# Row sums' reciprocals scheduled apart from GpSimd, and 32-bit value products for eight heads in the fills' PSUM banks

## The chip, the cores and the metric

The kernel runs on one core of one Trainium2 chip. The metric is the device time of one execution in microseconds; the kernel before is timed in three runs, and one execution of it is profiled. The engines are named as in the profile: PE (TensorE's matmuls) and PEld (its weight loads), DVE (VectorE), ACT (ScalarE), POOL (GpSimd), SP (SyncE, which issues the DMAs).

## The reference

Three layers follow one another: an attention with a decay per key, a mixture of eight experts whose gates are normalised by rows and columns, and a dense layer pair. All is in 32-bit floats.

```
# q, k, v: (4, 8, 576, 64); f: (4, 8, 576); 32 heads in all
scores = (q @ k.T) / 8 + cum[:, None] - cum[None, :]      # cum = cumsum(log(clip(f))), causal mask
attn   = exp(scores - rowmax);  attn /= attn.sum(-1) + 1e-9
x      = concat_heads(attn @ v)                           # (2304, 512)
P      = exp(x @ w_gate - max); 8 times: rows, then columns normalised     # (2304, 8)
x      = sum over e of P[:, e] * (relu(x @ w1[e]) @ w2[e])                 # w1: 512x1024, w2: 1024x512
h      = x @ w_in;  out = max(0.01 * h, h) @ w_out                         # 512x2048, 2048x512
```

## The kernel before

**Two stages.** The first 321 us or so are the head stage: 32 heads of attention, two heads (a pair) sharing a few steps. From there on PE runs the experts' and the dense layers' products in an order that a second planner writes out; that is the main stage. Products of the first experts on the tokens of the first heads, the *fills*, are already put between the heads' steps, four matmuls at a time (first layer L203, second layer L230). They go into the two PSUM banks of the pool `ps_m`.

**Precision.** Most products are split: an operand x is stored as a rounded high part hi (type fp32r) and a low part x - hi, and the product is made of two or three fast matmuls. "Native" products take the 32-bit values as they are, at more PE time a matmul.

**The steps of a head.** DVE casts q and k to their high parts (L393, L387), GpSimd makes the low parts (L398, L390). Scores go into the four banks of `ps_s` in six pieces (L441, L442). DVE masks each piece and takes the row minimum (L453, L457); ScalarE makes the exponentials with their row sums (L466). PE transposes the probabilities into the two banks of `ps_t` (L492); ScalarE copies them out (L499), and for split heads DVE subtracts to get the low part `ptl` (L508). The value product (`pv`, L528) comes in two pieces of columns, 0 to 255 and 256 to 575, into a bank of `ps_s`. For heads 0 to 9 (`n < EARLY`) it is native, with v as loaded (`rv`); for the others v is split (`vp`: DVE cast L423, GpSimd low part L425), and the product leaves the terms for ScalarE's copy (L549) and DVE's addition (L556) to join. Native heads need one ScalarE copy (L545).

**The reciprocal.** For a pair, `recip` (L570 to L572) runs three small DVE operations on the row sums: an addition on 96x2, the addition of 1e-9 on 128x10, a reciprocal on 128x10. GpSimd spreads the result (`rb`, L577), PE transposes that, DVE multiplies it onto the pair's output `xs` (L592), ScalarE and GpSimd split it (L607, L611), and the gate product follows (L637, L638). GpSimd also makes the low parts of the fills' weights (L164).

**The order.** `head_events` and the loop over the fills list every step with its engine, a duration in microseconds, a delay, what it needs, which PSUM ring it takes and when it is due. `run_heads` then walks a clock of its own and puts the steps of each engine into an order. The engine letters are M for PE, A for ScalarE, V for DVE, P for GpSimd, D for the DMA queue. A step marked "VP" runs on DVE and, like every step of GpSimd, is placed only where this clock has the other of the two engines free of such steps; a step marked "V" is placed without regard to GpSimd:

```
if how[0] in ("VP", "P"):
    s_ = max(s_, port["P" if e == "V" else "V"])
```

The casts (k1, q1, vp) are marked "VP", the reciprocal (rc) "V". The clock lives in the planner alone; on the chip each engine runs its own order and waits only for data and free buffers.

Of the kernel before, what the change touches and what calls it, by code (L numbers as in the profile page):

```python
# [10 lines left out]
F32 = mybir.dt.float32  # L11
# [9 lines left out]
P = 128  # L21
B, H, S, D = 4, 8, 576, 64
# [44 lines left out]

EARLY = 10
HEAD_E = dict(
# [25 lines left out]
def moe_kernel(ctx, tc, qT, kT, v, fg, w_gate, w1, w2, w_in, w_out, out):  # L95
# [198 lines left out]
    with ExitStack() as actx:  # L294
# [120 lines left out]
        def v_split(n, op):  # L415
            if n < EARLY:
                return
            rv = rvs[(n // 2) % 2]
            if op == "vp":
                vps[n] = a2.tile([P, 5, 4 * D], F32R, tag="vp", name="vp")  # L420
            vv = vps[n].rearrange("p j (s d) -> p j s d", d=D)
            if op == "vp":
                nc.vector.tensor_copy(vv[:, :, 0:4:3, :], rv)  # L423
            else:
                nc.gpsimd.tensor_tensor(  # L425
                    vv[:, :, 1:3, :], rv, f(vv[:, :, 0:4:3, :]), ALU.subtract)
# [54 lines left out]
        def tr(n, u):  # L481
            if n < EARLY:
                if n not in pts:
                    pts[n] = (a2.tile([P, PTW], F32, tag="pth", name="pt"),)
            elif n not in pts:
                pts[n] = (a2.tile([P, PTW], F32R, tag="pth", name="pth"),
                          a2.tile([P, PTW], F32R, tag="ptl", name="ptl"))
            ps = ps_t.tile([P, 512], F32, tag="t", name="ps_t")
            for j, qs, c in TPLAN[u]:
                for i in qs:  # L490
                    m = QT[i][1]
                    nc.tensor.transpose(  # L492
                        ps[:KV[j], c:c + m], prb[n, i][:m, j * P:j * P + KV[j]], ident[:m, :m])
                    c += m
            tps[n, u] = ps
# [6 lines left out]
        def tr_lo(n, u):  # L502
            if n < EARLY:
                return
            hi, lo = pts[n]
            for r, c0, c1, o in TEV[u]:
                w = slice(o, o + c1 - c0)
                nc.vector.tensor_tensor(  # L508
                    lo[:r, w], tps[n, u][:r, c0:c1], f(hi[:r, w]), ALU.subtract)
# [5 lines left out]
        def pv(n, r):  # L515
            ra, rb = RG[r]
            ps = ps_s.tile([P, 512], F32, tag="s", name="ps_pv")
            js = [j for j in range(5) if (QT[j][0] if j == 4 else j * P) < rb]
            todo = [(j, s) for j in js for s in pts[n]]
            for x, (j, s) in enumerate(todo):  # L520
                q0 = 480 if j == 4 else j * P
                a = max(ra, q0)
                o = PTOFF[j] + a - q0
                if n < EARLY:
                    vp = rvs[(n // 2) % 2][:KV[j], j].rearrange("p h d -> p (h d)")
                else:
                    vp = vps[n - n % 2].rearrange("p j (h c) -> p j h c", h=2)[:KV[j], j, n % 2]
                nc.tensor.matmul(  # L528
                    ps[:, a - ra:rb - ra], vp, s[:KV[j], o:o + rb - a],
                    start=(x == 0), stop=(x == len(todo) - 1))  # L530
            pvs[n, r] = ps
# [7 lines left out]
        def pv_copy(n, r):  # L539
            ra, rb = RG[r]  # L540
            me, ot = halves(n)
            if n // 2 not in xss:
                xss[n // 2] = a2.tile([P, S], F32, tag="xs", name="xs")
            if n < EARLY:
                nc.scalar.activation(  # L545
                    xss[n // 2][me, ra:rb], pvs.pop((n, r))[me, 0:rb - ra], AF.Copy)
                return
            xts[n, r] = a2.tile([P, 320], F32, tag="xt", name="xt")
            nc.scalar.activation(xts[n, r][me, 0:rb - ra], pvs[n, r][ot, 0:rb - ra], AF.Copy)  # L549

        def pv_add(n, r):
            if n < EARLY:
                return
            ra, rb = RG[r]
            me, ot = halves(n)
            nc.vector.tensor_tensor(  # L556
                xss[n // 2][me, ra:rb], pvs.pop((n, r))[me, 0:rb - ra],
                xts.pop((n, r))[me, 0:rb - ra], ALU.add)
# [97 lines left out]
        TE, TL = 6.9, 8.6  # L656
        base_of = [TE * min(n, EARLY) + TL * max(n - EARLY, 0) for n in range(NH + 8)]
        hvs = {}
        BUFS = dict(s=4, t=2, m=2, xt=2)

        def place(n, off):
            x = n + off
            k = int(x)
            return base_of[k] + (x - k) * (base_of[k + 1] - base_of[k]) if x > 0 else x * TE
# [24 lines left out]
        def head_events(n):  # L689
            early, pair = n < EARLY, n - n % 2  # L690
            T = HEAD_E if early else HEAD_T
# [11 lines left out]
            if n % 2 == 0:  # L703
                PT_ = PAIR_E if early else PAIR_T
                if n:
                    hv(("vload", n), ("D", 1.1, 2.0), v_load, n,
                       need=[("vl", n - 4)] + [("pv", n - m, r) for m in (4, 3) for r in range(2)])
                if not early:
# [4 lines left out]
            for x in (0, 1, 2, 3, 4, 5):  # L713
                hv(("qk", n, x), ("M", M_QK[x], 0.17), qk, n, x,
                   need=[(k, n) for k in ("rows", "k1", "k2", "q1", "qd", "q1l")]
                   + [("pv", n - 3, r) for r in range(2)],
                   ring="s", rel=[("ex", n, x), ("mn", n, x)], due=place(n, T[f"qk{x}"]))
                hv(("mn", n, x), ("V", V_MN[x], 0.12), qk_min, n, x,
# [15 lines left out]
            for r in range(2):  # L734
                hv(("pv", n, r), ("M", ((0.65, 2.4) if early else (0.44, 1.5))[r], 0.2), pv, n, r,
                   need=[(lo, n, u) for u in ((0, 1), (0, 1, 2, 3))[r]]
                   + [("vload", pair), ("vl", pair)],
                   ring="s", rel=[("cp" if early else "ad", n, r)], due=place(n, T[f"pv{r}"]))
                xfree = [(k, pair - 4) for k in ("xd", "xl")]
# [4 lines left out]
            if n % 2 == 0:  # L744
                return
            n, last = pair, "cp" if early else "ad"
            T = PT_ = PAIR_E if early else PAIR_T
            hv(("rc", n), ("V", 0.5, 0.1), recip, n,
               need=[("ex", n + y, x) for y in range(2) for x in range(6)])
# [11 lines left out]
            for r in range(2):  # L761
                hv(("ga", n, r), ("M", 0.3, 0.17), gate, n, r, need=[("xl", n), ("wg",)],
                   ring="t", rel=[("gb", n, r)], due=place(n, T[f"ga{r}"]))
                hv(("gb", n, r), ("V", 0.4, 0.07), gate_add, n, r, need=[("ga", n, r), ("gb", n - 2, r)])

# [7 lines left out]
        for x, (dur, fns) in enumerate(fills):  # L773
            for fn in fns:
# [22 lines left out]
                else:  # L797
# [7 lines left out]
                    if q == 0:  # L805
                        fowner = ("low", j, b, c) if not l2_ else ("end", j, b, c)
                    F = ("f", x)
                    hv(F, ("M", 0.88 if l2_ else 0.71, 0.2), fill_main, x, fn, need=list(dict.fromkeys(need)),
                       ring="m" if q == 0 else None, rel=[fowner], due=1e6 + x)
# [17 lines left out]
        def run_heads():  # L827
# [14 lines left out]
            must = set(rest)  # L842
            free = dict(M=0.0, A=0.0, V=0.0, P=0.0, D=0.0)
            port = dict(V=0.0, P=0.0)
# [13 lines left out]
            stop, owed = None, set()  # L858
            while must or owed:
                best = None  # L860
# [45 lines left out]
                if not must and not owed and fills[stop][1][0].args[3] < 2:  # L906
                    owed |= {fmain[stop + 1]} | set(fside[stop + 1])
                for y in succ[x]:
# [975 lines left out]
```

## Time and profile before

| | us |
|---|---|
| median of three runs (lowest, highest) | 2042.12 (2039.62 to 2042.59) |
| the profiled execution's own time | 2041.69 |
| its span, first to last instruction | 2039.9 |
| PE busy | 1996.0 (98%) |
| PEld busy | 1947.4 (95%) |
| DVE busy | 1767.0 (87%) |
| ACT busy | 981.2 (48%) |
| POOL busy | 1163.1 (57%) |

The shares are means over both stages; the stages differ, so each is read by itself. The span is 1.8 us shorter than the execution's own time. Matmuls overlap and their ends are modelled, so a busy PE is not a PE at its peak.

### The profile page before, as it was taken

Reading aid. Unit: us, or ns where it says so; the run is one execution under the profiler, and the core shown is the slowest. Engines: PE = TensorE matmul, PEld = TensorE weight load, DVE = VectorE, ACT = ScalarE, POOL = GpSimd, SP = SyncE. Lnnn points to the kernel's source line nnn. Section 1 sums busy time; section 2 is a strip of 40 time slices with the busy share of each in tenths; the row PEclk is TensorE's granted clock in tenths of the full one; section 3 lists DMA queues with packets and bytes.
Section 4 is the critical chain, followed back from the end, with each engine's and each line's share of the span. In section 5 each row is a group of like instructions: output and inputs, shape, how many; then the busy total and the mean of one; then the engine's idle time right before and its main releaser. Section 6 shows DMA issues by size and latency. Waiting matters only on the chain.

```text
span 2039.9 us, 32131 instructions
## 1 busy us (share of the span) xinstructions
PE 1996.0 (98%) x11600; PEld 1947.4 (95%) x11600; DVE 1767.0 (87%) x2426; ACT 981.2 (48%) x1752; POOL 1163.1 (57%) x731
## 2 busy tenths in 40 slices
PE   7999899999999999999999999999999999999999
PEld 5788788999999999999999999999999999999998
DVE  6799897688889999998989989889898988888766
ACT  6877675454444334433343343334334346655443
POOL 5667556446665657666566646656575564455302
PEclk9999999999999999999999999999999999999999
DMA  5645437567887767786767777777777755767563
GB/s 142 164 136 159 129 104 245 214 244 247 280 305 269 257 233 255 240 273 238 240 243 256 256 246 245 255 243 249 242 266 244 250 215 191 259 233 238 179 210 139
DMA packets 145622, 460.54 MB, mean 226 GB/s; under 512 B 15912, under 2 KB 42168, under 8 KB 145464
## 3 DMA queue, kind: packets, MB, share of 16 engines
q1 hardware_dynamic: 145460, 458.48, 66.8%
q8 instruction: 93, 1.52, 0.3%
q14 instruction: 65, 0.53, 0.1%
q10 hardware_dynamic: 4, 0.00, 0.0%
HBM read 402.76 MB, written 51.08 MB: 222 GB/s over the span
## 4 chain that ended last, share of the span: by engine, by line
PE 85%; DVE 8%; ACT 2%; DMA 2%; issue 2%; POOL 0%; SPq 0%; DVEq 0%; ACTq 0%; POOLq 0%
PE x L1382 43%; PE y L1382 32%; PE ps_pv L528 1%; PE ps_m L230 1%; PE ps_t L492 1%; PE y L230 1%; PE y L203 1%; DVE ps_s L453 1%; PE ps_s L441 1%; PE x L203 1%; PE x L230 1%; PE ps_s L442 1%; ACT p L466 1%; DVE hl L1453 1%; PE ps_m L203 1%
## 5 line engine op out<-in xcount | busy, mean ns | idle before, releaser
L1382 PE MATMUL x<-xw,w 128*128 128x384 f32 x2676 | 501.0, 335 | 2.7 <-DVE xw L1136 1.4
L1382 PE MATMUL x<-hh,w 128*128 128x384 f32 x1792 | 491.1, 334 | 2.7 <-DVE w L1204 1.7
L1382 PEld LDWEIGHTS x<-xw,w 128*128 128x128 f32 x2676 | 466.9, 188 | 4.9 <-DVE xw L1136 2.0
L1382 PE MATMUL y<-xw,w 128*128 128x384 f32 x2004 | 375.0, 335 | 0.9 <-DVE u L1424 0.9
L1382 PE MATMUL y<-hh,w 128*128 128x384 f32 x1344 | 368.1, 334 | 0.0
L1382 PEld LDWEIGHTS y<-xw,w 128*128 128x128 f32 x2004 | 349.5, 188 | 1.6 <-DVE u L1424 1.4
L1204 POOL TENSOR_TENSOR w<-wr,w 128x512 fp32r<-128x512 f32 x161 | 255.7, 1592 | 165.4 <-ACT w L160 152.7
L1382 PEld LDWEIGHTS x<-hh,w 128*128 128x128 f32 x1792 | 326.7, 188 | 3.6 <-DVE w L1204 2.4
L1382 PE MATMUL x<-hl,w 128*128 128x384 f32 x896 | 299.7, 335 | 0.9 <-DVE hl L1453 0.9
L1382 PEld LDWEIGHTS y<-hh,w 128*128 128x128 f32 x1344 | 245.2, 188 | 0.3 <-issue 0.3
L1382 PE MATMUL y<-hl,w 128*128 128x384 f32 x672 | 224.8, 334 | 0.0
L1465 DVE TENSOR_TENSOR acc_C<-x,acc_C 128x768 f32<-128x768 f32 x177 | 168.3, 951 | 32.3 <-PE x L1382 30.6
L1465 DVE TENSOR_TENSOR acc_C<-y,acc_C 128x768 f32<-128x768 f32 x148 | 140.9, 952 | 57.6 <-PE y L1382 56.1
L160 ACT ACTIVATE w<-wr 128x512 fp32r<-128x512 f32 x288 | 175.2, 622 | 28.6 <-PE y L1382 17.4
L1382 PEld LDWEIGHTS x<-hl,w 128*128 128x128 f32 x896 | 168.3, 188 | 1.5 <-DVE hl L1453 1.5
L1449 ACT ACTIVATE hh<-u 128x768 fp32r<-128x768 f32 x91 | 77.1, 847 | 142.4 <-PE y L1382 82.1
L1449 ACT ACTIVATE hh<-spare 128x768 fp32r<-128x768 f32 x84 | 71.1, 847 | 148.4 <-PE x L1382 62.6
L1449 ACT ACTIVATE hh<-k 128x768 fp32r<-128x768 f32 x112 | 94.9, 847 | 89.3 <-PE x L1382 50.2
L1382 PEld LDWEIGHTS y<-hl,w 128*128 128x128 f32 x672 | 126.1, 188 | 0.2 <-DVE hl L1453 0.2
L1449 ACT ACTIVATE hh<-c 128x768 fp32r<-128x768 f32 x70 | 59.3, 846 | 123.5 <-PE y L1382 83.4
L1418 ACT ACTIVATE u<-x 128x768 f32<-128x768 f32 x91 | 74.1, 814 | 92.0 <-PE x L1382 84.6
L1453 POOL TENSOR_TENSOR hl<-k,hh 128x768 fp32r<-128x768 f32 x35 | 69.0, 1973 | 83.3 <-ACT hh L1449 83.3
(253 smaller groups left out, 3848.8 us busy)
## 6 DMA issues: line engine op xcount, KB each, us to landing
xw<-xo_t SPq DMA_DIRECT2D x208, 768.0 KB
xw<-xo_b SPq DMA_DIRECT2D x154, 768.0 KB
wr<-in_w_dram SPq DMA_DIRECT2D x88, 512.0 KB
pb<-prow SPq DMA_DIRECT2D x44, 384.0 KB
xo_t<-xw SPq DMA_DIRECT2D x16, 768.0 KB
rq<-in_qT_dram SPq DMA_DIRECT2D x64, 144.0 KB
rk<-in_kT_dram SPq DMA_DIRECT2D x64, 144.0 KB
xo_b<-xw SPq DMA_DIRECT2D x12, 768.0 KB
```

The source lines that it names most:

```text
L160: nc.scalar.activation(hv, src, AF.Copy)
L203: nc.tensor.matmul(ps, w_[:, fs], x_[k][:, xs], start=(x == 0), stop=(x == 11))
L230: nc.tensor.matmul(ps, h_[:, ts], w_, start=(x == 0), stop=(x == 11))
L441: nc.tensor.matmul(o, q1[:, q0:q0 + m], k1[:, k0:k9], start=True, stop=False)
L442: nc.tensor.matmul(o, q2[0:D + 4, q0:q0 + m], k2[0:D + 4, k0:k9], start=False, stop=True)
L453: nc.vector.tensor_tensor_reduce(o, o, mask[:m, w:w + k9 - k0], scale=-SCALE, scalar=3e38, op0=ALU.add, op1=ALU.min, accum_out=mn)
L1204: ENG[e].tensor_tensor(lo, blk(g, which, WSRC[which][n]), f(hi), ALU.subtract)
L1382: nc.tensor.matmul(o_, w[:, k, w_], m[:, k, :], start=a and k + y == 0, stop=z and k == 1 and y == 2, skip_group_check=True)
L1418: nc.scalar.activation(ctile(u, name, name, bufs), pview(u, p), AF.Copy)
L1449: nc.scalar.activation(hi, tmp[u, LSRC[l]], AF.Copy)
L1453: ENG[e].tensor_tensor(lo, tmp[u, LSRC[l]], f(hi), ALU.subtract)
L1465: nc.vector.tensor_tensor(a, pview(u, l), a, ALU.add)
```

## The change

Five things are edited. `rc` becomes a "VP" step. The set of native heads becomes 0 to 7 (`NATIVE`), and their value products take a bank of `ps_m`, the fills' ring, where they took one of `ps_s`. The planner's numbers move: the fills' matmul steps cost 0.94 and 0.77 where they cost 0.88 and 0.71, the DMA queue and head 0's scores start at 1.5, the gate steps of the pairs that straddle two token parts get unequal durations. The need of `vload` is rewritten for pairs whose forerunner has no low part. And the loop goes on until a fill product is whole, so that the head stage ends on one.

```
-EARLY = 10
+NATIVE = (0, 1, 2, 3, 4, 5, 6, 7)
...
         def pv(n, r):
             ra, rb = RG[r]
-            ps = ps_s.tile([P, 512], F32, tag="s", name="ps_pv")
+            ps = ps_m.tile([P, 512], F32, tag="m", name="ps_m") if n in NATIVE else \
+                ps_s.tile([P, 512], F32, tag="s", name="ps_pv")
...
-                       need=[("vl", n - 4)] + [("pv", n - m, r) for m in (4, 3) for r in range(2)])
+                       need=[("pv", n - m, r) for m in (4, 3) for r in range(2)] if n - 4 in NATIVE
+                       else [("vl", n - 4)])
...
-                   ring="s", rel=[("cp" if early else "ad", n, r)], due=place(n, T[f"pv{r}"]))
+                   ring="m" if early else "s", rel=[("cp" if early else "ad", n, r)], due=place(n, T[f"pv{r}"]))
...
-            hv(("rc", n), ("V", 0.5, 0.1), recip, n,
+            hv(("rc", n), ("VP", 0.5, 0.1), recip, n,
...
-                    hv(F, ("M", 0.88 if l2_ else 0.71, 0.2), fill_main, x, fn, need=list(dict.fromkeys(need)),
+                    hv(F, ("M", 0.94 if l2_ else 0.77, 0.2), fill_main, x, fn, need=list(dict.fromkeys(need)),
...
-            free = dict(M=0.0, A=0.0, V=0.0, P=0.0, D=0.0)
+            free = dict(M=0.0, A=0.0, V=0.0, P=0.0, D=1.5)
...
-            while must or owed:
+            idle = []
+            while True:
+                if not must and not owed:
+                    if fills[stop][1][0].args[3] == 2:
+                        break
+                    owed |= {fmain[stop + 1]} | {m for m in fside[stop + 1] if m not in over}
```

Since the planner decides the order, these edits move instructions on every engine in the head stage. From the experts' first products on, PE's order is the same. Seven lines are added ahead of and among these functions, so that line numbers after the change are larger by one around `recip` (L571 to L573) and by seven in the main stage.

On DVE, around the reciprocal of the pair of heads 14 and 15: the cast of the next q (L393) stands right ahead of it, with one multiplication between.

```order
L453 ISA ps_s,st<-ps_s,mask 96x288
L453 ISA st 96x1
L393 CAST q_2042<-rq 128x576
L592 TENSOR_TENSOR xs<-xs,ps_r 128x320
L570 TENSOR_TENSOR st<-st 96x2
L571 TENSOR_SCALAR st<-st 128x10
L572 RECIPROCAL st<-st 128x10
L508 TENSOR_TENSOR ptl<-ps_t,pth 128x96
```

The same place in the changed kernel:

```order
L387 CAST k_2078<-rk 128x576
L508 TENSOR_TENSOR ptl<-ps_t,pth 128x512
L453 ISA ps_s,st<-ps_s,mask 96x512
L453 ISA st 96x1
L649 TENSOR_TENSOR lgT<-ps_g,lgT 16x384
L571 TENSOR_TENSOR st<-st 96x2
L572 TENSOR_SCALAR st<-st 128x10
L573 RECIPROCAL st<-st 128x10
L423 CAST vp<-rv_193 128x5x2x64
L508 TENSOR_TENSOR ptl<-ps_t,pth 128x96
```

The reciprocal now stands a subtraction, a masked minimum and a gate addition behind the last cast, which is that of k, and a cast of v follows it.

On GpSimd, the operations ahead of the spread (rb) of the same pair, before the change:

```order
L164 TENSOR_TENSOR w<-wr,w 128x512 x3
L398 TENSOR_TENSOR q_2042<-rq,q_2042 64x576
L611 TENSOR_TENSOR xp<-xs,xp 128x192
L611 TENSOR_TENSOR xtl<-xs,xth 128x384
L577 COPY rb<-st 128x640
L565 MEMSET st 128x30
L390 TENSOR_TENSOR k_1_228<-rk,k_2043 64x576
```

And in the changed kernel:

```order
L612 TENSOR_TENSOR xp<-xs,xp 128x192
L612 TENSOR_TENSOR xtl<-xs,xth 128x384
L398 TENSOR_TENSOR q_2077<-rq,q_2077 64x576
L164 TENSOR_TENSOR w<-wr,w 128x512
L390 TENSOR_TENSOR k_1_228<-rk,k_2078 64x576
L578 COPY rb<-st 128x640
L425 TENSOR_TENSOR vp<-rv_193,vp 128x5x128
L566 MEMSET st 128x30
L398 TENSOR_TENSOR q_2197<-rq,q_2197 64x576
```

The output's low part (xp, xtl) has moved ahead of the q low part, and the k low part from behind the spread to right ahead of it.

On PE, the value product of head 8 between the scores of head 9, before the change:

```order
L528 MATMUL ps_pv<-pt,rv_193 128x256
L528 MATMUL ps_pv<-pt,rv_193 128x128
L441 MATMUL ps_s<-k_1016,q_1015 128x384
L442 MATMUL ps_s<-k_1_228,q_1_226 128x384
L586 MATMUL ps_r<-ident,rb 128x128
L586 MATMUL ps_r<-ident,rb 128x96 x2
L492 MATMUL ps_t<-ident,p_1177 128x96
L492 MATMUL ps_t<-ident,p_1177 64x96
L441 MATMUL ps_s<-k_1016,q_1015 96x512
L442 MATMUL ps_s<-k_1_228,q_1_226 96x512
L528 MATMUL ps_pv<-pt,rv_193 128x320 x3
```

And in the changed kernel:

```order
L441 MATMUL ps_s<-k_1007,q_1006 128x384
L442 MATMUL ps_s<-k_1_228,q_1_226 128x384
L441 MATMUL ps_s<-k_1007,q_1006 96x512
L442 MATMUL ps_s<-k_1_228,q_1_226 96x512
L587 MATMUL ps_r<-ident,rb 128x128 x2
L529 MATMUL ps_pv<-pth,vp 128x256
L529 MATMUL ps_pv<-ptl,vp 128x256
L529 MATMUL ps_pv<-pth,vp 128x128
L529 MATMUL ps_pv<-ptl,vp 128x128
L587 MATMUL ps_r<-ident,rb 128x128
L587 MATMUL ps_r<-ident,rb 128x96 x2
L529 MATMUL ps_pv<-pth,vp 128x320
```

Head 8's product is now split into high and low parts, and all scores of head 9 stand ahead of it. Counted in the same two orders, the first-layer fill products ahead of head 12 are 28 in the changed kernel and 8 before; ahead of head 15 both have 48 of the first and 16 of the second layer; at the end of the head stage 192 stand against 204 of the first layer, and 144 of the second in both. None stands ahead of head 10 in either.

## Rows read from the trace of the kernel before

**Rows 1.** Windows by stage: length, busy us (instructions) by engine, clock, DMA share, GB/s.

```profile
20.00:96.00 76.00, 70.17 (x424) 57.10 (x422) 56.45 (x176) 57.49 (x189) 43.29 (x40) 0.98 0.53 144
96.00:321.00 225.00, 210.39 (x1363) 187.95 (x1362) 199.92 (x579) 163.64 (x478) 140.39 (x121) 0.98 0.47 133
321.00:2040.00 1719.00, 1706.49 (x9776) 1694.77 (x9776) 1497.76 (x1635) 749.09 (x1057) 969.89 (x552) 1.00 0.70 242
```

**Rows 2.** PE's waits, 20:96, 96:210 and 210:325 us: total us, times, longest.

```profile
PE ps_pv L528 <- ACT p L466: 4.7, 4, 2.0
...
PE ps_t L492 <- DVE ptl L508: 6.8, 5, 2.2
...
PE ps_t L492 <- DVE ptl L508: 4.0, 3, 2.1
PE ps_s L441 <- DVE xs L556: 2.3, 3, 1.7
```

**Rows 3.** DVE's groups by form, 20 to 310 us: count, busy us, mean ns.

```profile
L571 DVE TENSOR_SCALAR st<-st 128x10 f32<-128x10 f32 x16 | 14.3, 894 | 3.1 <-ACT p L466 1.9
...
L570 DVE TENSOR_TENSOR st<-st 96x2 f32<-96x2 f32 x16 | 13.9, 870 | 0.0
```

**Rows 4.** Timeline of 202 to 208 us: start, us, instruction, idle before.

```profile
202.23 1.42 POOL L398 TENSOR_TENSOR q<-rq,q 64x576 fp32r<-64x576 f32 x1 [0.55 <-ACT xth L607]
...
202.44 1.22 DVE L570 TENSOR_TENSOR st<-st 96x2 f32<-96x2 f32 x1
...
203.72 1.42 POOL L611 TENSOR_TENSOR xtl<-xs,xth 128x576 fp32r<-128x576 f32 x1
203.76 1.41 DVE L571 TENSOR_SCALAR st<-st 128x10 f32<-128x10 f32 x1
...
206.68 0.89 PE L492 MATMUL ps_t<-ident,p 128*128 128x128 f32 x7 [1.74 <-DVE ptl L508]
```

**Rows 5.** DVE's timeline, 183.5 to 187 us.

```profile
183.94 0.15 DVE L570 TENSOR_TENSOR st<-st 96x2 f32<-96x2 f32 x1
184.19 0.17 DVE L571 TENSOR_SCALAR st<-st 128x10 f32<-128x10 f32 x1
```

**Rows 6.** Windows around the first and the last of four slow stretches.

```profile
43.30:47.00 3.70, 3.60 (x14) 2.95 (x15) 1.90 (x8) 3.12 (x13) 0.00 (x0) 0.69 0.29 83
286.00:290.00 4.00, 4.00 (x22) 3.90 (x21) 3.10 (x11) 2.46 (x9) 1.69 (x2) 0.64 0.05 19
```

**Rows 7.** PE's timeline: a native value product, then first and last of a split one.

```profile
92.27 0.92 PE L528 MATMUL ps_pv<-pt,rv 128*128 128x256 f32 x4
93.94 2.52 PE L528 MATMUL ps_pv<-pt,rv 128*128 128x320 f32 x10
...
111.70 0.28 PE L528 MATMUL ps_pv<-pth,vp 128*128 128x256 f32 x1
...
111.99 0.28 PE L528 MATMUL ps_pv<-ptl,vp 128*128 128x128 f32 x1
113.97 0.31 PE L528 MATMUL ps_pv<-pth,vp 128*128 128x320 f32 x1
...
115.29 0.27 PE L528 MATMUL ps_pv<-ptl,vp 64*128 64x96 f32 x1
```

**Rows 8.** DVE's groups of split heads, 96 to 321 us.

```profile
L508 DVE TENSOR_TENSOR ptl<-ps_t,pth 128x480 fp32r<-128x480 f32 (+4 forms) x108 | 49.6, 489 | 3.0 <-ACT pth L499 2.4
L556 DVE TENSOR_TENSOR xs<-ps_pv,xt 64x256 f32<-64x256 f32 (+1 forms) x44 | 19.7, 451 | 2.2 <-ACT xt L549 1.5
L423 DVE CAST vp<-rv 128x640 fp32r<-128x640 f32 x10 | 8.1, 810 | 2.3 <-DMA rv<-in_v_dram 2.0 <-issue 0.3
```

**Rows 9.** Windows of the pairs of heads 8, 18 and 20, between their first scores.

```profile
72.25:87.86 15.61, 14.67 (x93) 12.09 (x92) 11.22 (x38) 13.31 (x43) 12.76 (x12) 1.00 0.63 174
163.16:183.01 19.85, 18.57 (x125) 16.62 (x124) 18.86 (x57) 15.69 (x47) 15.20 (x15) 1.00 0.45 130
183.01:201.51 18.50, 18.50 (x121) 16.09 (x120) 16.92 (x54) 14.52 (x45) 14.40 (x12) 1.00 0.61 177
```

More of the change, by code (lines that the diff above doesn't have):

```diff
@@ L415, in v_split @@
         def v_split(n, op):
-            if n < EARLY:
+            if n in NATIVE:
                 return
@@ L481, in tr @@
         def tr(n, u):
-            if n < EARLY:
+            if n in NATIVE:
                 if n not in pts:
@@ L502, in tr_lo @@
         def tr_lo(n, u):
-            if n < EARLY:
+            if n in NATIVE:
                 return
@@ L523, in pv @@
                 o = PTOFF[j] + a - q0
-                if n < EARLY:
+                if n in NATIVE:
                     vp = rvs[(n // 2) % 2][:KV[j], j].rearrange("p h d -> p (h d)")
@@ L543, in pv_copy @@
                 xss[n // 2] = a2.tile([P, S], F32, tag="xs", name="xs")
-            if n < EARLY:
+            if n in NATIVE:
                 nc.scalar.activation(
@@ L551, in pv_add @@
         def pv_add(n, r):
-            if n < EARLY:
+            if n in NATIVE:
                 return
@@ L656, in moe_kernel @@
         TE, TL = 6.9, 8.6
-        base_of = [TE * min(n, EARLY) + TL * max(n - EARLY, 0) for n in range(NH + 8)]
+        base_of = [TE * min(n, 10) + TL * max(n - 10, 0) for n in range(NH + 8)]
         hvs = {}
@@ L689, in head_events @@
         def head_events(n):
-            early, pair = n < EARLY, n - n % 2
+            early, pair = n in NATIVE, n - n % 2
             T = HEAD_E if early else HEAD_T
@@ L716, in head_events @@
                    + [("pv", n - 3, r) for r in range(2)],
-                   ring="s", rel=[("ex", n, x), ("mn", n, x)], due=place(n, T[f"qk{x}"]))
+                   ring="s", rel=[("ex", n, x), ("mn", n, x)], due=place(n, T[f"qk{x}"]),
+                   t=0.0 if n else 1.5)
                 hv(("mn", n, x), ("V", V_MN[x], 0.12), qk_min, n, x,
@@ L761, in head_events @@
             for r in range(2):
-                hv(("ga", n, r), ("M", 0.3, 0.17), gate, n, r, need=[("xl", n), ("wg",)],
+                w = 0.3 if n // 8 != 1 else (0.2, 0.42)[r]
+                hv(("ga", n, r), ("M", w, 0.17), gate, n, r, need=[("xl", n), ("wg",)],
                    ring="t", rel=[("gb", n, r)], due=place(n, T[f"ga{r}"]))
-                hv(("gb", n, r), ("V", 0.4, 0.07), gate_add, n, r, need=[("ga", n, r), ("gb", n - 2, r)])
+                hv(("gb", n, r), ("V", w + 0.08, 0.07), gate_add, n, r, need=[("ga", n, r), ("gb", n - 2, r)])
         hv(("wg",), ("V", 1.2, 0.1), gate_prep, t=20.0)
@@ L905, in run_heads @@
                     owed |= {m for m in fside[stop] if m not in over}
-                if not must and not owed and fills[stop][1][0].args[3] < 2:
-                    owed |= {fmain[stop + 1]} | set(fside[stop + 1])
                 for y in succ[x]:
```

## The prediction

> **What bounds the kernel now.** I read the stages first. In the main stage from 321 us on, TensorE (PE) is busy 1706.49 of 1719.00 us; the change leaves the order of that stage's work alone apart from its first microseconds, so I expect nothing from it. In the head stage, 20 to 321 us, PE is idle 5.8 of 76 us and 14.6 of 225 us, and there VectorE (DVE) is the other full engine: 199.92 of 225 us, 89%, against 74% in the first ten heads [rows 1]. The reader is to see that only some 20 us of idle PE, and what a slow clock adds, can be won.
>
> Next the waits of PE inside that stage. From 96 us on two kinds carry nearly everything: transposes that need a ps_t bank and wait for DVE's low-part subtraction (6.8 us in 5 waits, 4.0 us in 3), and score products that wait for DVE's xs addition (2.3 us). Before 96 us it is the value product waiting for ScalarE's exponentials, 4.7 us in 4 waits [rows 2]. So PE waits for a DVE that is late, but only some fifteen times: something makes DVE late at particular places.
>
> DVE by form shows what. The row sums' reciprocal is three tiny operations a head pair. Its addition on 96x2 takes 870 ns on average, its scalar addition on 128x10 takes 894 ns [rows 3]; where nothing disturbs them they take 0.15 and 0.17 us [rows 5]. All 16 pairs together: 13.9 + 14.3 = 28.2 us against 16 x 0.32 = 5.1 us, so 23.1 us of DVE are stall. The timeline shows the cause: GpSimd (POOL) starts L398 at 202.23 and holds it to 203.65; DVE's L570 starts at 202.44 and ends at 203.66. POOL's next operation runs 203.72 to 205.14, DVE's L571 203.76 to 205.17. Each waits out the rest of a GpSimd operation, and PE stands still for 1.74 us, up to 206.68, behind the DVE work queued there [rows 4]. Where the reciprocal meets no GpSimd operation [rows 5], the two heads around it have PE busy for all of their 18.50 us, while the pair before has 1.3 us of idle PE and needs 19.85 us [rows 9].
>
> [...]
>
> **The clock.** [...] Half speed over 3.5 us costs up to 1.75 us, four times 7.0 us.
>
> **The change, part by part.** *Reciprocals apart from GpSimd.* The scheduler now places the reciprocal only where its own clock has GpSimd free. Of before, 13 of 16 reciprocals stand at most 0.5 us of DVE work behind a q or k cast, and that cast is what releases the 1.4 us operations on POOL. In the changed order 14 of 16 have at least 1.8 us of DVE work between, and the GpSimd operation ahead of the spread (rb) is normally done when the reciprocal comes. What the stalls cost PE now: 6.8 + 4.0 + 2.3 = 13.1 us [rows 2], 2.0 us of the early 4.7 (the longest of those waits, right behind a reciprocal), and 7.0 us of clock: 22.1 us. Not all comes back. Nothing but the schedule's own clock holds the two engines apart, since no semaphore stands between them, and in about six pairs free-running weight splits (L164) stand between the casts and rb on POOL. I take six tenths, 13.3 us; the bounds are one third (7) and all (22).
>
> *Eight native heads instead of ten.* Heads 8 and 9 get the split value product. PE: the native product takes 0.92 + 2.52 us a head, the split one 0.57 (111.70 to 112.27) + 1.59 (113.97 to 115.56) [rows 7], so 1.28 us less, 2.6 us for both heads. DVE: five L508 of 489 ns and two L556 of 451 ns a head, one L423 of 810 ns for the pair [rows 8]: 2 x 3.35 + 0.81 = 7.5 us more. That pair now takes 15.61 us with DVE busy 11.22 [rows 9]. With 18.7 us of DVE work, at the 95% that heads 18 and 19 reach [rows 9], it needs 19.7 us: 4.1 us longer. Against that, the fills start sooner in head terms: 28 fill products stand ahead of head 12 instead of 8, and by head 15 both orders have done the same 64, so what is lost at heads 8 and 9 is mostly PE time that later heads have less need of. I take +1 us, bounds -2.6 and +4.1.
>
> *Value products in the fills' banks.* Score products of heads 0 to 7 get all four ps_s banks, and the product no longer waits for an exponential to free its bank. That can return what is left of the 4.7 us, 2.7 us [rows 2]; but the transposes behind need the same exponentials, so I take -1 (0 to -2.7). No fill product stands ahead of head 10 in the new order, so the two uses of ps_m hardly meet. If that cover fails, a fill step waits for one ScalarE copy of the product.
>
> *The rest* (start times of DMA and head 0, fill costs of 0.94 and 0.77, the end at a whole fill, gate weights, the vload condition) only moves the order. The head stage ends with 12 fill products fewer (192 instead of 204 of the first layer); they run right behind it, where PE is full, so they cost the same. I take 0, bounds plus and minus 2.
>
> **Sum.** -13.3 + 1 - 1 = -13.3 us on the profiled execution's 2041.69 us (span 2039.9): 2028.4. It stands 0.4 us below the median of 2042.12, so on the median 2029 us, 0.65% faster. About 0.2%, 4 us, is what a measurement of this kernel can tell from no change.
>
> **Rivals.** [...]
>
> *DVE becomes the bound.* The time freed goes to the extra 7.5 us of heads 8 and 9, and the split heads run at DVE's pace; taking 7 us from the reciprocals, +4.1 for the pair and -1 for the banks gives 2038. For it speaks DVE's 89% in the heads [rows 1]; against it that this 89% holds the 23 us of stalls.
>
> *The collisions only move.* Other operations of GpSimd, the weight splits above all, meet the reciprocal at its new place; or the cast behind it is the one that stalls. Then the change does not do what it says: 2040 to 2043 us.
>
> *Slower: GpSimd stands behind rb.* POOL works in order. The spread rb waits for the reciprocal, which now comes up to some 8 us of DVE work after the last cast, and behind rb stand the statistics' memset and the next q and k low parts, which the next score products need. If that holds each of 13 pairs by 1.5 us beyond GpSimd's slack, 19.5 us are lost against 13.3 gained: 2048 us. It decides from about 1 us a pair on. Against it speaks that POOL is idle 85 of 225 us in this stage [rows 1].
>
> **How the numbers follow.** The forecast, a gain of 8 to 19 us, 0.67; everything back 0.09; DVE the bound 0.10; collisions moved 0.08; slower 0.06. The first two and some 0.06 of the third, which lies about at the bound, are faster by over 0.2%, together 0.82; within it lie 0.04 + 0.08 = 0.12; slower 0.06. The range runs from 2020 (all returned) to 2038 (DVE the bound), with one microsecond above for the moved order: 2039. It leaves out collisions moved, slower, and half of everything back, 0.08 + 0.06 + 0.04.
>
> **What would show it right or wrong.** Right: the two tiny operations of the reciprocal fall from about 0.88 to under 0.4 us on average; PE's waits for ptl fall from 10.8 to under 4 us; at least three of the four slow-clock stretches are gone; the main stage lasts as long as before; heads 8 and 9 take 18 to 20 us. Wrong: the tiny operations stay above 0.6 us (collisions moved); DVE over 93% busy with PE still waiting for ptl (DVE the bound); PE's score products waiting for GpSimd's q and k low parts (the queue behind rb).

## The result, and the profile after

The changed kernel takes 2022.85 us (median of four runs, 2022.32 to 2025.89) where the kernel before takes 2042.36 on the same chip (2039.62 to 2042.70): a ratio of 0.991, interval 0.9893 to 0.9928, 19.5 us less. The forecast was 2029, in a range of 2020 to 2039; direction and mechanism hold, and the gain was put too low by 6 us. One execution of e5 below (4216.16 us) and one of the kernel before beside it (3975.93 us) took twice as long as all others and stand in no ratio. The profiled execution took 2022.56 us, its span 2020.7, which is the page's first part:

```profile
span 2020.7 us, 32150 instructions
...
PE 1989.1 (98%) x11600; PEld 1941.3 (96%) x11600; DVE 1749.1 (87%) x2441; ACT 979.7 (48%) x1752; POOL 1164.9 (58%) x732
```

Windows of the changed kernel by stage, with the columns of [rows 1]; the head stage now ends at about 301 us:

```profile
20.00:96.00 76.00, 73.41 (x472) 62.14 (x471) 58.35 (x209) 62.97 (x204) 50.03 (x44) 1.00 0.63 168
96.00:301.00 205.00, 198.64 (x1303) 175.18 (x1302) 180.00 (x565) 154.86 (x459) 135.76 (x115) 1.00 0.50 138
301.00:2020.70 1719.70, 1707.13 (x9784) 1695.60 (x9783) 1497.53 (x1631) 750.06 (x1060) 968.99 (x553) 1.00 0.70 242
```

Everything was won in the head stage. PE is idle 2.59 + 6.36 = 9.0 us from 20 us to its end where it was 20.4 [rows 1], 11.5 us less; it is busy 272.05 us where it was 280.56, 8.5 us less. In these 8.5 are the slow clock (the granted clock of the two windows is 1.00, not 0.98, and none of the four slow stretches, at most 7.0 us, is left), the 12 fill products that moved behind the stage (12 x 0.175 us = 2.1) and the shorter products of heads 8 and 9 (2.6 by the prediction's rows). These add up to 11.7, so that the clock's own part, what the other two leave, may be nearer to 4 us; ends of matmuls are modelled in the trace, and it cannot be told closer. The main stage is as long as before, 1719.70 against 1719.00 us. The 0.175 us are the spacing of the last twelve fill products of the kernel before, which take 2.25 us with the last one's own 0.33 among them:

```profile
316.22 2.25 PE L203 MATMUL ps_m<-xp,w 128*128 128x384 f32 x12
```

A fifth slow stretch, which the prediction did not count, has stayed in this execution: the kernel before has one from 320 to 324 us (0.65), where the head stage ends, and the changed kernel one at the same point of its work (its second trace, e9, has none):

```profile
300.00:304.00 4.00, 4.00 (x16) 4.00 (x16) 0.80 (x5) 0.46 (x2) 0.00 (x0) 0.57 1.01 335
```

PE's waits in the changed kernel, from 20 to 96, 96 to 210 and 210 to 303 us, with "..." between the stretches and for lines left out (total us, times, longest):

```profile
PE ps_r L587 <- DVE ptl L508: 0.8, 1, 0.8
PE ps_s L441 <- ACT p L466: 0.8, 3, 0.3
PE ps_t L492 <- DVE ptl L508: 0.5, 1, 0.5
...
PE ps_s L441 <- ACT p L466: 2.3, 3, 1.4
PE ps_t L492 <- DVE lgT L649: 1.3, 2, 0.6
PE ps_g L638 <- DVE ptl L508: 0.4, 1, 0.4
PE ps_t L492 <- ACT p L466: 0.2, 1, 0.2
PE ps_t L492 <- DVE ptl L508: 0.2, 1, 0.2
...
PE ps_s L441 <- DVE xs L557: 0.2, 1, 0.2
```

The waits for ptl, 6.8 + 4.0 us in [rows 2], are 0.8 + 0.5 + 0.4 + 0.2 = 1.9 us; those for xs fall from 2.3 to 0.2 from 96 us on. The early value products no longer wait for an exponential. No score product waits for a low part from GpSimd.

DVE's groups by form, 15 to 310 us, the reciprocal's operations (compare [rows 3]):

```profile
L573 DVE RECIPROCAL st<-st 128x10 f32<-128x10 f32 x16 | 3.5, 217 | 0.6
L572 DVE TENSOR_SCALAR st<-st 128x10 f32<-128x10 f32 x16 | 2.8, 173 | 0.7
...
L571 DVE TENSOR_TENSOR st<-st 96x2 f32<-96x2 f32 x16 | 2.7, 166 | 0.1
```

Both small operations now take 166 and 173 ns, in all 16 pairs together 5.5 us instead of 28.2. The stall is gone to within 0.4 us. The timeline around one of them, at 120 us (start, us, instruction, idle before):

```profile
120.16 1.43 POOL L390 TENSOR_TENSOR k<-rk,k 64x576 fp32r<-64x576 f32 x1 [1.84 <-PE ps_t L492]
...
121.67 0.15 DVE L571 TENSOR_TENSOR st<-st 96x2 f32<-96x2 f32 x1
121.85 0.17 DVE L572 TENSOR_SCALAR st<-st 128x10 f32<-128x10 f32 x1
122.06 0.22 DVE L573 RECIPROCAL st<-st 128x10 f32<-128x10 f32 x1
...
122.41 0.72 POOL L578 COPY rb<-st 128x640 f32<-128x640 f32 x1 [0.83 <-PE ps_s L441]
```

GpSimd's k low part ends at 121.59 us and the addition starts 0.08 us later; the spread comes next. A margin that small held in this order. In others, below, it did not (e4, e8 and, about half as much, e5).

### The profile page after: what moved, and what is told of

It is laid out like the page before. It is cut to its first block, busy times and chain, and to the rows that moved or that the text cites. A ratio compares the mean times of both kernels' runs of the same rounds, so it can differ in the third digit from the quotient of the medians.

```text
span 2020.7 us, 32150 instructions
## 1 busy us (share of the span) xinstructions
PE 1989.1 (98%) x11600; PEld 1941.3 (96%) x11600; DVE 1749.1 (87%) x2441; ACT 979.7 (48%) x1752; POOL 1164.9 (58%) x732
## 4 chain that ended last, share of the span: by engine, by line
PE 86%; DVE 6%; DMA 3%; issue 2%; ACT 1%; POOL 1%; SPq 0%; DVEq 0%; POOLq 0%; ACTq 0%
PE x L1389 43%; PE y L1389 33%; DMA wr<-in_w_dram 2%; PE ps_t L492 1%; PE ps_pv L529 1%; PE ps_s L441 1%; PE ps_s L442 1%; PE ps_m L529 1%; PE ps_m L203 1%; PE ps_m L230 1%; PE x L230 1%; DVE hl L1460 1%; PE y L230 1%; DVE ps_s L453 0%; POOL w L164 0%
```

## The experiments

The theories. **A**: the two small operations are held by GpSimd's running operation because of the kind of operation they are, and their stall (23.1 us of DVE) is nearly all that the change removes. **B**: the stall is only a sign of DVE being full, and the gain comes from the other edits or from the new order. Intervals are of the ratio to the kernel before, run on the same chip; its medians were 2043.09 us (9 runs) beside e1 to e4, 2040.24 (11) beside e5 to e8 and 2040.58 (7) beside e9 to e12.

**e1: the kernel before with the reciprocal's step alone changed.**

```
-            hv(("rc", n), ("V", 0.5, 0.1), recip, n,
+            hv(("rc", n), ("VP", 0.5, 0.1), recip, n,
```

> The kernel before with the reciprocal's step marked VP and nothing else. Theory A (the stall behind GpSimd is nearly the whole gain): the reciprocal's two small operations fall from 0.88 to below 0.3 us on average and the time falls by 15 to 20 us, to 2022 to 2027 us. Theory B (eight native heads and the fills' banks carry about half of the gain, since heads 0 to 15 alone became 11.8 us shorter): the operations fall as well, but the time only by 6 to 11 us, to 2031 to 2036 us.

Measured: 2020.28 us, ratio 0.9889 (0.9876 to 0.9903), 22.8 us less. DVE's groups of this kernel:

```profile
L570 DVE TENSOR_TENSOR st<-st 96x2 f32<-96x2 f32 x16 | 3.5, 217 | 0.0
...
L571 DVE TENSOR_SCALAR st<-st 128x10 f32<-128x10 f32 x16 | 2.8, 173 | 0.7
```

One word in the planner's table does all that the whole change does; the time lies 2 us below theory A's range and 11 below B's. The order that the word draws brings back the whole 22.1 us that the prediction had counted as the stalls' cost, not six tenths of it.

**e2: the whole change without that word.**

```
-            hv(("rc", n), ("VP", 0.5, 0.1), recip, n,
+            hv(("rc", n), ("V", 0.5, 0.1), recip, n,
```

> The changed kernel with the reciprocal's step marked V again, all else kept. Theory A: the stalls come back (over 0.7 us an operation) and the time is 2036 to 2043 us. Theory B: the stalls come back, but heads and banks keep half of the gain: 2029 to 2035 us.

Measured: 2035.70 us, ratio 0.9968 (0.9956 to 0.9981), 7.4 us less. Its DVE groups:

```profile
L572 DVE TENSOR_SCALAR st<-st 128x10 f32<-128x10 f32 x16 | 12.1, 755 | 2.0 <-ACT p L466 0.6
...
L571 DVE TENSOR_TENSOR st<-st 96x2 f32<-96x2 f32 x16 | 10.8, 677 | 0.0
```

The time lies between the two ranges. The other edits gain something by themselves, but 5.3 us of stall are gone in this order too (22.9 us in these two rows instead of 28.2), so they are not a clean measure of edits beside the stall. The two parts do not add up: 7.4 + 22.8 is 30.2, and both together give 19.5.

**e3: the kernel before in its own order, with another kind of operation.** The addition of two columns becomes a reduction over one input, and the addition of 1e-9 is left out. Nothing is moved: the step keeps its "V", its place and its planned duration.

```
-            nc.vector.tensor_tensor(st[:m, 0, 4], st[:m, 2, 2], st[:m, 2, 3], ALU.add)
-            nc.vector.tensor_scalar(rs, rs, EPS, None, ALU.add)
+            nc.vector.tensor_reduce(
+                st[:m, 0, 4], st[:m, 2, 2:4].rearrange("p j h -> p h j"), axis=AX.X, op=ALU.add)
```

> The kernel before, its order kept, with the reciprocal's two stalled operations replaced: the addition of two columns becomes a reduction over one input, and the addition of 1e-9 to the row sums is left out. [...] If the stall hangs on the place in the order and not on the kind of operation, the reduction takes 0.8 to 1.0 us too; only the dropped addition is saved, and the time falls by 3 to 10 us, to 2032 to 2039 us.

Measured: 2022.51 us, ratio 0.9903 (0.9888 to 0.9918), 20.6 us less. The reduction among DVE's groups:

```profile
L570 DVE TENSOR_REDUCE st<-st 96x2 f32<-96x4 f32 x16 | 2.3, 145 | 0.0
```

The timeline of this kernel at the pair that stands in [rows 4]:

```profile
189.66 1.42 POOL L398 TENSOR_TENSOR q<-rq,q 64x576 fp32r<-64x576 f32 x1 [0.55 <-ACT xth L607]
...
189.87 0.15 DVE L570 TENSOR_REDUCE st<-st 96x2 f32<-96x4 f32 x1
190.12 0.22 DVE L572 RECIPROCAL st<-st 128x10 f32<-128x10 f32 x1
...
190.73 0.15 DVE L457 TENSOR_TENSOR st<-st,ps_s 96x1 f32<-96x1 f32 x1
```

This separates A from B. The same GpSimd operation runs from 189.66 to 191.08 at the same place; the reduction and the reciprocal start and finish inside it, where the addition of [rows 4] was held to its end. In 12 of the 16 pairs the reduction ran beside a GpSimd operation, and none was held. So it is the kind of operation, and not how much DVE or GpSimd have to do: on average the held addition takes 870 ns and the held scalar addition 894 [rows 3], the reduction 145. The leaving out of one small operation a pair is no rival for 20.6 us: undisturbed it takes 0.17 us, 16 times 2.8 us.

The last line narrows it further. L457, the minimum of two row minima, is a tensor_tensor as the held addition is and about as small, but one of its inputs lies in PSUM. It takes 150 to 153 ns in all 32 heads of the kernel before, in 17 of them wholly within the time of GpSimd's two-input operations, and is never held. So the name of the operation does not decide it either: of two small tensor_tensors only the one with both inputs in SBUF is held.

PE's waits of this trace from 20 to 300 us hold none for ptl (10.8 us before); the largest is

```profile
PE ps_s L441 <- DVE xs L556: 2.0, 3, 1.2
```

and no window of 4 us in this stretch has a granted clock under 0.97. The profiled execution is the fastest of the four (2017.26 us at a mean clock of 1.000; the others 2022.17 to 2024.08 at 0.997 to 0.998), so what the other three still waited for is not shown.

**e4: the changed kernel with ten native heads.**

```
-NATIVE = (0, 1, 2, 3, 4, 5, 6, 7)
+NATIVE = tuple(range(10))
```

> The changed kernel with ten native heads instead of eight, their value products in the fills' banks. By the prediction's term the split of heads 8 and 9 costs 1 us (between -2.6 and 4.1), so this is 2019 to 2025.5 us against 2022.85. Theory B, by which eight heads carry a part of the gain: 2028 us or more.

Measured: 2032.65 us, ratio 0.9953 (0.9941 to 0.9966), 8.8 us above the change by the ratios (0.0043), 9.8 by the medians. The expectation by the prediction's term missed this by 7 us or more; it lies where theory B had it. In this order "VP" does not keep the engines apart:

```profile
L572 DVE TENSOR_SCALAR st<-st 128x10 f32<-128x10 f32 x16 | 6.8, 425 | 0.9
...
L571 DVE TENSOR_TENSOR st<-st 96x2 f32<-96x2 f32 x16 | 5.3, 329 | 0.0
```

12.1 us instead of 16 x 0.32 = 5.1, so 7.0 us of stall, suggested itself as the reason. **e7** tried that reason: the same kernel with e3's reduction (1e-9 left out), which was not held there.

```
-NATIVE = (0, 1, 2, 3, 4, 5, 6, 7)
+NATIVE = tuple(range(10))
...
-            nc.vector.tensor_tensor(st[:m, 0, 4], st[:m, 2, 2], st[:m, 2, 3], ALU.add)
-            nc.vector.tensor_scalar(rs, rs, EPS, None, ALU.add)
+            nc.vector.tensor_reduce(
+                st[:m, 0, 4], st[:m, 2, 2:4].rearrange("p j h -> p h j"), axis=AX.X, op=ALU.add)
```

> The kernel with ten native heads in the fills' banks (2032.65 us), its order kept, with the reciprocal's addition made as a reduction over one input and the addition of 1e-9 left out. There the reciprocal's operations took 0.33 and 0.43 us on average, 7 us of stall in all, although marked VP. If these stalls are why ten heads cost 10 us more than eight, the time falls by 6 to 10 us, to 2022 to 2027 us. If two more native heads cost PE and fills themselves, it falls by 3 us at most, to 2030 us or more.

Measured: 2030.25 us, ratio 0.9957 (0.9944 to 0.9971). With no stall left (the reduction takes 143 ns) it is no faster than e4 by the ratios, so the stall was not the main reason. What e7's trace does show is one long chain at 184 to 191 us. ScalarE's longest wait from 180 to 195 us (total us, times, longest):

```profile
ACT w L160 <- DMA wr<-in_w_dram: 4.7, 2, 3.8
```

The timeline of ScalarE and of the two engines behind it (start, us, instruction, idle before):

```profile
188.43 0.63 ACT L160 ACTIVATE w<-wr 128x512 fp32r<-128x512 f32 x1 [3.85 <-DMA wr<-in_w_dram]
188.96 0.98 ACT L499 ACTIVATE pth<-ps_t 128x480 fp32r<-128x480 f32 x2
189.55 1.19 DVE L508 TENSOR_TENSOR ptl<-ps_t,pth 128x480 fp32r<-128x480 f32 x2 [2.97 <-ACT pth L499]
...
190.35 0.74 PE L492 MATMUL ps_t<-ident,p 128*128 128x128 f32 x5 [3.24 <-DVE ptl L508]
```

A fill weight's copy stands on ScalarE's queue before its transfer has landed; the rounding of the transposed exponentials waits behind it, then DVE's subtraction, then PE for 3.24 us. The list of waits would call this "PE waits for DVE", as it does the stalls of [rows 2]; only DVE's own idle time ahead of L508 (2.97 us, released by ScalarE) tells the two apart. The windows of e7 behind that wait (columns of [rows 1]) show the clock:

```profile
188.00:192.00 4.00, 1.65 (x10) 1.59 (x10) 2.20 (x6) 3.57 (x12) 1.27 (x1) 0.84 0.07 17
192.00:196.00 4.00, 4.00 (x21) 3.48 (x21) 3.00 (x10) 2.42 (x8) 1.27 (x1) 0.73 0.01 2
```

So the chain is worth 3.2 us of waiting and, at 0.84 and 0.73 over 8 us, up to 1.7 us of clock (4 x 0.16 + 4 x 0.27): about half of the 9.6 to 11.4 us by which e7's ratio lies above the change's (0.9957 against 0.991 and 0.9901). The chain stands in e4's trace too:

```profile
190.29 0.63 ACT L160 ACTIVATE w<-wr 128x512 fp32r<-128x512 f32 x1 [4.23 <-DMA wr<-in_w_dram]
...
192.21 0.63 PE L492 MATMUL ps_t<-ident,p 128*128 128x128 f32 x5 [3.77 <-DVE ptl L508]
```

In the two traces of the change, its own and e9's, ScalarE waits at most 2.0 and 2.2 us for such a transfer, and PE at most 0.8 us for ptl. Why ten heads bring the chain was not tried, and what makes up the rest was not found. A rival is open as well: e4 and e7 put the products of heads 8 and 9 into the fills' banks, where the kernel before has them in the scores'; ten heads in the scores' banks were not run in this order.

**e5: the changed kernel with the native value products back in the scores' banks.**

```
-            ps = ps_m.tile([P, 512], F32, tag="m", name="ps_m") if n in NATIVE else \
-                ps_s.tile([P, 512], F32, tag="s", name="ps_pv")
+            ps = ps_s.tile([P, 512], F32, tag="s", name="ps_pv")
...
-                   ring="m" if early else "s", rel=[("cp" if early else "ad", n, r)], due=place(n, T[f"pv{r}"]))
+                   ring="s", rel=[("cp" if early else "ad", n, r)], due=place(n, T[f"pv{r}"]))
```

> The changed kernel with the eight native heads' value products back in the score banks. By the prediction's term the fills' banks are worth 1 us (0 to 2.7): 2023 to 2026 us. If they are what made heads 2 to 8 run with hardly any lost PE time (7.3 us sooner at head 8 than before), this is 2028 to 2031 us.

Measured: 2020.01 us, ratio 0.9902 (0.9888 to 0.9917). The banks are worth nothing that shows at the end. Head 8's first score starts at 66.06 us here and at 64.95 in the changed kernel, so the 1 us that the prediction gave them is there at that point, and lost again by the stage's end. The small operations take 244 and 268 ns here, 3.1 us of stall, and the time is none the longer for it.

**e6: e2 with e3's reduction**, the changed kernel with "V" and an addition that is not held (1e-9 left out).

```
-            nc.vector.tensor_tensor(st[:m, 0, 4], st[:m, 2, 2], st[:m, 2, 3], ALU.add)
-            nc.vector.tensor_scalar(rs, rs, EPS, None, ALU.add)
+            nc.vector.tensor_reduce(
+                st[:m, 0, 4], st[:m, 2, 2:4].rearrange("p j h -> p h j"), axis=AX.X, op=ALU.add)
...
-            hv(("rc", n), ("VP", 0.5, 0.1), recip, n,
+            hv(("rc", n), ("V", 0.5, 0.1), recip, n,
```

> The changed kernel with the reciprocal marked V again, but its addition made as a reduction over one input and the addition of 1e-9 left out. [...] If the V order itself is the worse one, for reasons other than the stall, it stays at 2030 us or more.

Measured: 2029.09 us, ratio 0.9941 (0.9928 to 0.9954), 0.9 us under the 2030 that a worse order was expected to keep, and between e2 (2035.70 us) and the change (2022.85 and 2021.03 us). Against e2's 0.9968, removing 17.8 us of stall gains 0.0027, 5.5 us; the order that "VP" draws is another 6 to 8 us faster (0.9901 to 0.991). In this order waits for ptl of 2.3 us remain, the longest of 1.6 us, and a slow clock behind that one:

```profile
80.00:84.00 4.00, 2.41 (x18) 2.04 (x17) 3.94 (x12) 3.09 (x8) 3.50 (x4) 0.94 0.35 111
84.00:88.00 4.00, 4.00 (x21) 3.60 (x19) 2.92 (x10) 2.09 (x7) 1.34 (x2) 0.63 0.01 2
```

The same wait stands in e2 (1.80 us at 87.11), beside small operations of 0.15 and 0.17 us. It is no stall: DVE is busy for 3.94 of the 4 us in the first of these windows, late with work of its own. So in the changed kernel's order "VP" does two things: it keeps the stall away, and it draws an order that is better for other reasons; by these ratios the second is worth no less than the first.

**e8: the changed kernel with the old fill costs.**

```
-                    hv(F, ("M", 0.94 if l2_ else 0.77, 0.2), fill_main, x, fn, need=list(dict.fromkeys(need)),
+                    hv(F, ("M", 0.88 if l2_ else 0.71, 0.2), fill_main, x, fn, need=list(dict.fromkeys(need)),
```

> The changed kernel with the planner's old durations for fill steps, 0.88 and 0.71. The prediction took the planner's numbers at nothing, within 2 us: 2021 to 2025 us. If every new order draws its own collisions, as ten heads did, it can lie anywhere from 2019 to 2033 us, and the reciprocal's operations tell which: each 1 us of their stall shows as 0.7 to 1 us of time.

Measured: 2026.15 us, ratio 0.9937 (0.9925 to 0.9949): 0.0027 to 0.0036 above the change's two ratios, 5.5 to 7.3 us (3.3 and 5.1 by the medians). Against the change's second ratio, below, the intervals part at 0.9925 and 0.9916; against its first they overlap by 0.0003. The profiled execution is the slowest of five (2031.25 us; the others 2024.56 to 2026.72). In it the small operations take 414 and 285 ns, 6.1 us of stall. That the stall is what costs is not shown: PE's three longest waits, 2.1, 2.2 and 2.5 us at 95.75, 127.85 and 207.08 us, each stand behind a weight copy on ScalarE that waited 2.1 to 2.8 us for its transfer, as in e7, and ahead of the second and the third an addition of the reciprocal is held as well (0.99 and 1.23 us). The second of them:

```profile
126.23 0.63 ACT L160 ACTIVATE w<-wr 128x512 fp32r<-128x512 f32 x1 [2.78 <-DMA wr<-in_w_dram]
...
127.85 0.48 PE L441 MATMUL ps_s<-k,q 128*96 128x512 f32 x1 [2.17 <-ACT p L466]
```

The planner's costs move nothing on an engine by themselves; they decide the order, and with it whether "VP" holds and where a copy meets a transfer that has not landed.

**e9 to e12**, on one chip: e9 is the changed kernel again, e10 is e1 again, and the next two start from it. e11 adds e3's reduction to e1 (1e-9 left out):

```
-            nc.vector.tensor_tensor(st[:m, 0, 4], st[:m, 2, 2], st[:m, 2, 3], ALU.add)
-            nc.vector.tensor_scalar(rs, rs, EPS, None, ALU.add)
+            nc.vector.tensor_reduce(
+                st[:m, 0, 4], st[:m, 2, 2:4].rearrange("p j h -> p h j"), axis=AX.X, op=ALU.add)
```

and e12 adds eight native heads to e1, with the heads' planned starts kept:

```
-EARLY = 10
+EARLY = 8
...
-        base_of = [TE * min(n, EARLY) + TL * max(n - EARLY, 0) for n in range(NH + 8)]
+        base_of = [TE * min(n, 10) + TL * max(n - 10, 0) for n in range(NH + 8)]
```

> The changed kernel itself, beside the three runs below on one chip. 2021 to 2025 us, 0.9 to 1.0% below the kernel before.

> The kernel before with the reciprocal marked VP alone, once more, now on the same chip as the changed kernel. If the other edits cost what the first comparison suggests, it is 2 to 4 us faster than the changed kernel; if they are worth nothing either way, the two agree within 1.5 us; by the prediction's terms (+1 and -1 us) they agree.

> The same kernel (VP alone), its order kept, with the addition made as a reduction over one input and the addition of 1e-9 left out (row sums are at least 1, where it changes nothing). VP alone left 1.1 us of stall in 16 pairs and 2.8 us for the dropped additions: if every microsecond of VectorE in the head stage were worth one of time, it would gain 3 to 4 us, to about 2016 to 2018 us; if VectorE is no longer what PE waits for, it gains nothing that can be told, 2019 to 2021 us.

> The kernel before with the reciprocal marked VP and eight native heads instead of ten, value products in the score banks, all the planner's other numbers as before. By the prediction's term eight heads cost 1 us (-2.6 to 4.1): 2018 to 2025 us. If the order that happens to come out decides more than the heads' work, it can be 5 to 10 us off, and then PE's waits name other steps than the reciprocal's.

```
                                     median us (range)             ratio (interval)
e9   the change again                2021.03 (2018.96 - 2021.37)   0.9901 (0.9886 - 0.9916)
e10  "VP" alone again                2017.86 (2016.81 - 2022.13)   0.9894 (0.9878 - 0.9911)
e11  "VP" alone, reduction           2020.53 (2018.46 - 2022.88)   0.9901 (0.9886 - 0.9916)
e12  "VP" alone, eight native heads  2022.54 (2021.37 - 2023.69)   0.9910 (0.9896 - 0.9925)
```

All four intervals overlap. "VP" alone has the lower median both times, 2.6 us below the change in the first comparison and 3.2 in the second (4.3 and 1.4 us by the ratios), which is too little to call it faster; that the other edits help beside it is not shown by any run. e11 has 4.2 us less of small DVE work than e10 and is not faster. That PE no longer waits for that work is likely and not shown, since e11's trace has a wait that e10's does not have, and a gain of this size could hide behind it:

```profile
136.72 0.34 PE L442 MATMUL ps_s<-k,q 68*96 68x288 f32 x1 [2.75 <-DMA rk<-in_kT_dram]
```

## Why the prediction was right in direction and short in size

**The mechanism held.** Stalled operations, a late DVE, PE's waits for ptl and xs, then a slow clock: e3 cuts the chain at its first link, with the order untouched, and gets 20.6 of the 22.1 us that the prediction had read from the waits and the clock. The expected sign on the two small operations came (0.17 us, forecast under 0.4), that on the ptl waits (1.9 us, under 4), that on the slow stretches (all four gone, at least three forecast) and that on the main stage.

**The step that failed is "I take six tenths, 13.3 us".** Measured alone the term is 22.8 us (e1), or 20.6 with the order kept (e3): the bound "all (22)" was the value. The reason for the discount was that "nothing but the schedule's own clock holds the two engines apart", so that collisions would come back. In e1's order and in the change's they hardly do: 1.1 us of stall is left in the one (16 x (0.217 + 0.173 - 0.32)) and 0.3 in the other. The worry itself was sound: with the same "VP", e4 keeps 7.0 us, e8 6.1 and e5 3.1. It was a property of the order at hand, and the order could be looked at. The prediction had counted that 14 of 16 reciprocals stand clear of the casts, which was evidence for nearly all coming back, and then set it aside for a general doubt. Everything back, 2020 us with a chance of 0.09, came nearer than the forecast.

The 7.0 us of clock in the 22.1 are four times half speed over 3.5 us, an upper bound. The trace of the kernel before has a granted clock of 0.50 in each of the four slow stretches, of which [rows 6] has the first and the last (columns of [rows 1]):

```profile
45.00:48.00 3.00, 3.00 (x9) 2.08 (x7) 2.16 (x7) 2.19 (x9) 0.38 (x1) 0.50 0.01 3
209.00:211.50 2.50, 2.50 (x10) 2.40 (x9) 2.50 (x10) 1.74 (x6) 1.29 (x2) 0.50 0.07 15
229.50:232.00 2.50, 2.50 (x13) 2.30 (x12) 2.32 (x9) 2.21 (x10) 0.17 (x1) 0.50 0.00 0
287.50:290.00 2.50, 2.50 (x13) 2.40 (x13) 1.63 (x6) 1.22 (x6) 0.19 (x1) 0.50 0.00 0
```

Windows of 0.5 us over each whole stretch put 1 - clock, summed, at 1.7 us each, 6.8 in all. No run shows that all 7.0 us came back: what PE is busy for less in the changed kernel leaves the clock's own part nearer to 4 us.

**Eight heads instead of ten: +1, about right in the sum and wrong in place.** Heads 8 and 9 take 14.39 us, not the 18 to 20 forecast: that DVE would set their pace was the wrong step. Windows of the changed kernel from head 0's first score to head 8's, then over heads 8 and 9, then over heads 10 and 11 (columns of [rows 1]):

```profile
8.33:64.95 56.62, 54.33 (x324) 45.36 (x325) 39.89 (x146) 44.31 (x149) 32.42 (x29) 1.00 0.61 164
64.95:79.34 14.39, 13.67 (x92) 11.54 (x92) 11.16 (x41) 13.72 (x42) 12.59 (x11) 1.00 0.79 210
79.34:98.33 18.99, 17.62 (x121) 15.80 (x121) 17.20 (x56) 14.40 (x45) 12.44 (x11) 1.00 0.64 164
```

Between the first scores of heads 8 and 10 DVE is busy for 11.16 of 14.39 us, no more than the 11.22 of [rows 9]; its added work falls into heads 10 and 11, 17.20 of 18.99 us. Heads 8 to 11 took 28.90 us before and take 33.38, 4.5 more, with 28 fill products instead of 8 among them. The 20 are 3.5 us at their spacing of 0.175 us and 4.5 by PE's busy time in them (6.20 against 1.74), which leaves 0 to +1.0, with all the other edits in it. The pair of heads 8 and 9 itself is 1.2 us shorter than before (15.61 in [rows 9]); heads 10 and 11 are 1 to 2 us longer beside the fill products. Put on "VP" alone, eight heads are 4.7 us slower by the medians (e12 against e10), just above the upper bound of 4.1, and their intervals overlap. In the change's order ten heads are the slower by some 9 us (e4), with the products of heads 8 and 9 in the fills' banks. What this edit is worth depends on the order around it.

**Value products in the fills' banks: -1.** It is there at head 8 (1.1 us, e5) and not at the end. Its bound of nothing holds for the whole kernel.

**"The rest ... I take 0, bounds plus and minus 2"** was too narrow. The fill costs alone are worth 3 to 7 us (e8), through the order they draw. Taken together, the edits beside "VP" come to about +3 us by medians and +1.4 to +4.3 by ratios (e1 against the change, e10 against e9), where the prediction had 0; that is the part of the sum which hid some of the first term's error, and it is not resolved by the intervals.

**The rivals.** DVE does not become the bound: it is busy 180.00 of 205 us, 88%, nearly what it was, yet PE waits for ptl 1.9 us, and less DVE work gains nothing that shows (e11). High share and no waits go together here, because the old share held 23 us of stall, and DVE's own work is now done in a shorter stage. The collisions did not move. GpSimd's queue behind the spread is not in PE's list of waits.

**What a microsecond of stall is worth** was not one number. Removing it by the reduction returned 20.6 us for 23.1 in the order of before (e3), 5.5 for 17.8 in the change's order with "V" (e6 against e2), and nothing that shows for 7.0 with ten heads (e7 against e4) or for 1.4 on "VP" alone (e11 against e10). Why the first order pays nine tenths and the second three tenths was not settled; the waits that stay in e6 are for exponentials (5.1 us), ptl (2.3) and xs (1.9), spread over the stage.

## What to carry to other kernels

A very short VectorE operation can cost a whole GpSimd operation: here a scalar addition of 0.17 us took 1.41 beside one of 1.42 us [rows 4]. Compare each small operation's mean with its undisturbed duration in the same trace, and where it is several times longer, look at what GpSimd does at that moment. There are two remedies: place it between GpSimd's operations, which holds only as long as the order and the planner's clock do (7.0 us of stall are there again in e4), or use a form that is not held, which needs no placing: here a reduction over one input (145 ns), while a scalar addition, which has one input too, was held (894 ns). To tell an engine that is held from one that is full, change the kind of operation and keep the order. Where a planner draws the order, an edit's worth cannot be added to another's: here a planner's cost that no engine ever sees moved the time by 3 to 7 us, and the same edit was worth 23 us alone and 13 beside the others, so time each edit alone and in company.

## What the runs showed of the hardware

A reduction from 96x4 to 96x2 and a reciprocal on 128x10, both small and in SBUF, ran at 145 and 216 ns beside running GpSimd operations; the reciprocal is at 216 or 217 ns on average in the traces of both kernels and of e1 to e8. A tensor_tensor on 96x1 with one input in SBUF and one in PSUM was not held either, 150 to 153 ns in all 32 of the kernel before. Two held operations in a row did not share one wait. GpSimd's next operation started 0.04 us ahead of the second, and each lost to one of its own [rows 4]: 1.22 + 1.41 us where 0.32 is the undisturbed time, 2.3 us for one reciprocal. So here DVE waited for more than data and free buffers: both additions had started, and ended 0.01 and 0.03 us behind the GpSimd operation that ran. One operation also lost to two: in e4 (and once in e8) a scalar addition stood through two operations of GpSimd, 2.78 us, so what is left of one operation, as the prediction has it, is no upper bound:

```profile
218.78 1.41 POOL L390 TENSOR_TENSOR k<-rk,k 64x576 fp32r<-64x576 f32 x1 [1.39 <-PE ps_t L492]
218.82 2.78 DVE L572 TENSOR_SCALAR st<-st 128x10 f32<-128x10 f32 x1
...
220.15 1.42 POOL L612 TENSOR_TENSOR xtl<-xs,xth 128x576 fp32r<-128x576 f32 x1
```

And a wait of PE of only 1.6 us was followed by a granted clock of 0.63 over 4 us (e6), up to 1.5 us (4 x 0.37) more by estimate, so that wait was paid for again after it had ended.
